# Three-part kernel on one core: 320-long sums in eight full-array passes, and the code for rare inputs moved behind the last block

## The chip, the core and the metric

The kernel runs on one core of a Trainium2 chip. Times are device microseconds from launch to the end of the slowest core, which is the only one here; a profile gives the times of each instruction in one execution, counted from its first instruction. The engines are TensorE (PE; its weight loads are listed as PEld), VectorE (DVE), ScalarE (ACT), GpSimd (POOL) and SyncE (SP), which issues most of the transfers.

## What is computed

Three parts follow each other. A gated linear attention over 4 sequences of 768 tokens gives 3072 rows of 320 numbers. Then a layer of 8 experts works on those rows whose skip score is positive: each such row goes to one expert. Last, a mixture layer takes the maximum of three products and multiplies it with a fourth matrix.

```python
def _moe_ref(x, w_skip, w_gate, w1, w2):          # x: 3072 x 320
    do_compute = x @ w_skip > 0
    xc = x[do_compute]
    e_idx = argmax(xc @ w_gate)                    # 8 experts
    ...
    h = np.maximum(xc[mask] @ w1[e], 0.0)          # 320 -> 1024
    y[mask] = gate_w[mask, None] * (h @ w2[e])     # 1024 -> 320
    out[do_compute] = xc + y

def _moe2_ref(x, w1, w2, w3, w_out):
    h = np.maximum(np.maximum(x @ w1, x @ w2), x @ w3)   # 320 -> 768
    return h @ w_out                                     # 768 -> 320
```

Both first layers, that of the experts and that of the mixture, are sums over 320 numbers. These are the sums that the change rewrites.

## The kernel before

Every factor is split into a high part and a low part (xH and xL, wH and wL), and a product is made of three: high by high, low weights by high, high weights by low. TensorE adds over 128 rows in one pass, so 320 is two chunks of 128 and a rest of 64. The weights hold the rest twice, in rows 0 to 63 and 64 to 127 of chunk 2. `x_parts` puts the high part of the rest of the tokens into rows 0 to 63 of chunk 2 and its low part into rows 64 to 127, so that one pass over 128 rows gives two of the three products of the rest. For the third, `terms` returns a short product of 64 rows: on rows 0 to 63, or, where `odd` is set, on rows 64 to 127, for which `x_parts` writes a second copy of the high part into a fourth chunk (line 264). So a sum is seven passes over 128 rows and one over 64.

The order is written out by hand; each engine takes its instructions in the order of the program. In `mixed_block` (line 308 for all these passes) the sums come in pairs: the first of a pair ends with its short pass, the second begins with its own, so that the two short passes stand next to each other on different halves of the rows and write different PSUM banks (tags pd and ps). In `experts`, `l1` does the same for two slabs of weights, with four short passes in the middle (line 423; the full ones are line 419). A call of `mixed_block` makes 18 sums (six slices f of 128 columns, three matrices), then the second layer (lines 323 to 325). Behind a sum, `post` handles what is finished of the slice before, and through `between` it places the transposes for the next tokens (lines 261 and 262) there, four times in a block that has another behind it: twice between the two sums of a pair, once between two pairs, once in the second layer.

The stages, by the profile: the attention, with one mixture block of 256 tokens (tile ext) woven into its end; eight experts of 256 rows each; a last step of 128 rows for the fullest expert (`few1`, then its second layer `l2`); a mixture block of 256 tokens (tile fx); five mixture blocks of 512 tokens (tiles fxH and fxL).

Between that last step and the mixture block on fx stands code that only some inputs need (lines 574 to 583): each of the five engines reads a number (`cnt_i`, line 574) and jumps over it where the number is zero (line 575), as with these inputs. Where the code is skipped, each engine still carries out a few semaphore instructions, which bring the semaphores to where they would stand behind it; these have line 575 too. `final` then loads the tokens of the first 512-wide blocks (line 273, on SP's queue).

Of the kernel before, what the change touches and what calls it, by code (L numbers as in the profile page):

```python
# [12 lines left out]
I32 = mybir.dt.int32  # L13
# [35 lines left out]
def build(tc, tp, kp, og, gates, w9, w1, w2, m1, m2, out):  # L49
    nc = tc.nc  # L50
    with ExitStack() as top:
# [24 lines left out]
        final(k, top, mp, wts)  # L76
# [167 lines left out]
def terms(xH, xL, wH, wL, c, odd):  # L244

    out = []
    for q in range(2):
        out += [(wH[:, q, c], xH[:, q]), (wH[:, q, c], xL[:, q]), (wL[:, q, c], xH[:, q])]  # L250

    out.append((wH[:, 2, c], xH[:, 2]))
    return out, ((wL[64:128, 2, c], xH[64:128, 3]) if odd else (wL[0:64, 2, c], xH[0:64, 2]))


def x_parts(k, x, xH, xL, c, bank="tr"):

# [6 lines left out]
    nc.scalar.copy(xH[64:128, 3, c], pt[0:64, 2])  # L264
# [11 lines left out]
def mixed_block(k, mp, x, xt, T, tile, between=None, apart=True):  # L276
# [22 lines left out]
    for f in range(6):  # L299
        c = slice(128 * f, 128 * f + 128)  # L300
        ps = []
        for m in range(3):
            p = k.bank("acc", [128, T])
            odd = (3 * f + m) % 2
            tt, short = terms(*xt, mp.H[m], mp.L[m], c, odd)
            tt = [short] + tt if odd else tt + [short]
            for i, (w, z) in enumerate(tt):
                nc.tensor.matmul(p, w, z, start=i == 0, stop=i == len(tt) - 1)  # L308
            ps.append(p)
            post()  # L310
            if m == 2:
                done.append((f, ps))
            yield
# [74 lines left out]

def experts(k, wts, mp):
    tc, nc = k.tc, k.nc  # L390
    X, XT, HT, l1s = {}, {}, {}, []
# [11 lines left out]
    def xprep(e, j):  # L403
        if j == 0:
            XT[e] = (p2.tile([128, 4, ST], F32R, name="xH"), p2.tile([128, 2, ST], F32R, name="xL"))
# [23 lines left out]

    def few1(e, s, xt):  # L430

        odd = s % 2 == 1
        ps = k.bank("acc", [128, SLAB])
        tt, short = terms(*xt, *wts.h1[e, s], slice(0, SLAB), odd)
        tt = [short] + tt if odd else tt + [short]
        for i, (w, x) in enumerate(tt):
            nc.tensor.matmul(ps, x[:, 0:128], w, start=i == 0, stop=i == len(tt) - 1)
        r = p2.tile([128, RW], F32, tag="y", name="r")
        nc.scalar.activation(r[:, 0:SLAB], ps, AF.Relu)
        yield  # L440
        pt = k.bank("tr", [128, 2, 128])
        for f in range(2):
            nc.tensor.transpose(pt[:, f], r[:, 128 * f : 128 * f + 128], k.ident)
        h = hp.tile([128, 2, ST], F32R, tag="hH", name="hH")[:, :, 0:128]
        g = hp.tile([128, 2, ST], F32R, tag="hL", name="hL")[:, :, 0:128]
        nc.scalar.copy(h, pt)
        nc.vector.tensor_sub(g, pt, h.bitcast(F32))
        yield h, g

    def l2(e, hs, c, xrow, apart=True):  # L450

        py = k.bank("row", [128, DM])
        for s in range(4):
            (hH, hL), (wH, wL) = hs[s], wts.h2[e, s]
            for f in range(2):
                a = s == 0 and f == 0
                z = s == 3 and f == 1
                nc.tensor.matmul(py, hH[:, f, c], wH[:, f], start=a, stop=False)
                nc.tensor.matmul(py, hH[:, f, c], wL[:, f], start=False, stop=False)
                nc.tensor.matmul(py, hL[:, f, c], wH[:, f], start=False, stop=z)  # L460
        y = p2.tile([128, RW], F32, tag="y", name="y")
        nc.scalar.copy(y[:, DM:RW], xrow[:, DM:RW])
        nc.vector.scalar_tensor_tensor(y[:, 0:DM], py, xrow[:, GTC : GTC + 1], xrow[:, 0:DM], ALU.mult, ALU.add)  # L463
        ins = nc.gpsimd.indirect_dma_start(  # L464
            k.table, bass.IndirectOffsetOnAxis(ap=xrow.bitcast(I32)[:, PLC : PLC + 1], axis=0), y, None,
            bounds_check=ROWS - 1, oob_is_err=False)
        if apart:
            k.apart(ins, "y", "y", "xl", "last", "pad")

    def more(e, n):  # L470

        with tc.If(n > ST):
            nc.sync.dma_start(k.table[bass.ds(n + e * CAP, 128)], k.zrow)
            for s in range(4):
                wts.raw1(e, s)
                wts.split1(e, s)
            for s in range(4):
                wts.raw2(e, s)
                wts.split2(e, s)
            with tc.For_i(ST, n, 128) as i:  # L480
                xo = p2.tile([128, 2, RW], F32, tag="xb", bufs=3, name="xo")[:, 0]
                nc.sync.dma_start(xo, k.table[bass.ds(i + e * CAP, 128)])
                xt = p2.tile([128, 4, ST], F32R, name="xH"), p2.tile([128, 2, ST], F32R, name="xL")
                x_parts(k, xo, *xt, slice(0, 128))
                hs = []
                for s in range(4):
                    *_, h = few1(e, s, xt)
                    hs.append(h)
                l2(e, hs, slice(0, 128), xo, apart=False)
# [13 lines left out]
    xt = wts.early = [wts.pool[2].tile([128, n, T1], F32R, name=f"fx{n}") for n in (4, 2)]  # L503
    wts.ahead1()
    counts = counted(k)
    for e in range(E + 1):
# [23 lines left out]
        for s in range(4):  # L530
            if e < E:
                HT[e, s] = l1(e, s, XT[e])
            else:
                last = few1(e, s, XT[e])
# [18 lines left out]
        for j in range(nj):  # L553
            l2(e, [HT[e, s] for s in range(4)], slice(128 * j, 128 * j + 128), X[e][:, j])
# [7 lines left out]
    def redo():  # L562

        x = p2.tile([128, 2, RW], F32, tag="xb", bufs=3, name="xo")[:, :, 0:MW]
        mixed_load(k, x, 0, T1)
        mixed_load(k, fx, T1, T1)
        x0 = p2.tile([128, 4, ST], F32R, name="xH"), p2.tile([128, 2, ST], F32R, name="xL")
        for j in range(2):
            x_parts(k, x[:, j], *x0, slice(128 * j, 128 * j + 128))
            x_parts(k, fx[:, j], *xt, slice(128 * j, 128 * j + 128))  # L570
        for _ in mixed_block(k, mp, x, x0, T1, early_tiles(wts, p2), apart=False):
            pass

    rare = nc.values_load(k.cnt_i[0:1, E + 4 : E + 5], min_val=0, max_val=N)
    with tc.If(rare > 0):
        left = nc.values_load(k.cnt_i[0:1, E + 2 : E + 3], min_val=0, max_val=N)
        with tc.If(left > 1):
# [811 lines left out]
```

## Time and profile before

| | us |
|---|---|
| median of 3 runs | 621.68 (618.18 to 624.29) |
| profiled execution, its own time | 618.2 |
| its span, first to last instruction | 616.5 |
| TensorE busy | 584.5 (95%) |
| VectorE, GpSimd, ScalarE busy | 323.9, 261.2, 255.5 |

The profiled execution is at the fast end of the three runs. The mean granted clock of TensorE was 0.987 of its full 2.4 GHz. A pass of TensorE is listed with its whole passage through the array, so that two passes that follow each other overlap in the list; what counts is the distance from one start to the next. A row of the timeline that ends in x2 stands for two passes of one kind.

### The profile page before, as it was taken

What the parts mean: (1) busy time and instruction counts of PE and PEld (TensorE: products, weight loads), DVE (VectorE), ACT (ScalarE), POOL (GpSimd) and SP (SyncE); (2) the same over time, 40 slices, a digit from 0 to 9 for tenths busy, and PEclk for the clock granted to TensorE, in tenths of its full rate; (3) what the DMA queues carried; (4) which work ended last, traced back from release to release, by engine and by line L of the source; (5) the groups of instructions that cost most, each with busy time, mean ns of one, the idle gap of its engine ahead of it and who ended that gap; (6) DMA issues with size and microseconds to landing.
All of it is one profiled execution on the core that took longest, in us unless ns stands there. A gap on an engine that the chain in (4) does not pass through costs nothing. (4 is left out here: it accounts for less than half of the span.)

```text
span 616.5 us, 11321 instructions
## 1 busy us (share of the span) xinstructions
PE 584.5 (95%) x4187; PEld 492.2 (80%) x4187; DVE 323.9 (53%) x792; ACT 255.5 (41%) x563; POOL 261.2 (42%) x281
## 2 busy tenths in 40 slices
PE   7979798899999999999999799999999999999994
PEld 3867687778888999999999687687688778678774
DVE  7889898998976477766666132231230321231220
ACT  4563646464634666666666132231232232222211
POOL 4346576777756555555553112213223123223222
PEclk9999998989999999999999899999999999999998
DMA  8587886787534677777763200002002002001001
GB/s 272 186 286 240 280 258 197 255 263 242 168 107 144 203 247 225 215 230 228 225 208 112 94 2 22 1 1 85 2 0 86 0 1 86 0 1 44 1 0 44
DMA packets 40857, 81.09 MB, mean 132 GB/s; under 512 B 6750, under 2 KB 21983, under 8 KB 40792
## 3 DMA queue, kind: packets, MB, share of 16 engines
q1 hardware_dynamic: 29608, 61.37, 31.5%
q10 hardware_dynamic: 8064, 9.05, 4.9%
q0 software_dynamic: 3120, 9.85, 4.2%
q8 instruction: 36, 0.59, 0.4%
q14 instruction: 29, 0.24, 0.1%
HBM read 66.68 MB, written 14.43 MB: 132 GB/s over the span
## 5 line engine op out<-in xcount | busy, mean ns | idle before, releaser
L287 POOL TENSOR_TENSOR hL<-t,hH 128x512 fp32r<-128x512 f32 x30 | 38.6, 1287 | 148.0 <-ACT hH L286 148.0
L308 PE MATMUL ps<-fxH,mH 128*128 128x512 f32 x135 | 57.7, 428 | 0.0
L308 PE MATMUL ps<-fxH,mL 64*128 64x512 f32 x135 | 57.6, 427 | 0.0
L308 PE MATMUL pd<-fxH,mL 128*128 128x512 f32 x135 | 57.5, 426 | 0.0
L286 ACT CAST hH<-t 128x512 fp32r<-128x512 f32 x30 | 18.6, 621 | 92.3 <-DVE t L296 92.3
L961 PE MATMUL pv<-KP,W 128*128 128x123 f32 (+2 forms) x384 | 53.1, 282 | 0.3 <-DVE xs L968 0.2
L308 PE MATMUL pd<-fxH,mH 128*128 128x512 f32 x135 | 52.9, 392 | 0.0
L961 PEld LDWEIGHTS pv<-KP,W 128*128 128x128 f32 x384 | 47.9, 193 | 3.5 <-DVE xs L968 0.7
L295 DVE TENSOR_TENSOR t<-t,ps 128x512 f32<-128x512 f32 x15 | 10.3, 688 | 65.0 <-PE ps L308 64.9
L981 POOL TENSOR_TENSOR g<-O,den 128x320 f32<-128x320 f32 x24 | 19.3, 804 | 52.6 <-DVE den L978 38.9
L308 PEld LDWEIGHTS pd<-fxH,mL 128*128 128x128 f32 x135 | 25.1, 186 | 19.5 <-issue 15.9
L887 ACT ACTIVATE W<-pd 128x512 f32<-128x512 f32 x48 | 27.6, 591 | 25.9 <-PE pd L886 19.4
L464 POOL DMA_INDIRECT table<-y,xb x17 | 16.7, 985 | 48.8 <-DVE y L463 37.5
L308 PEld LDWEIGHTS ps<-fxH,mH 128*128 128x128 f32 x135 | 25.3, 187 | 15.0 <-issue 11.0
L896 PE MATMUL ps<-TP 64*128 64x128 f32 x384 | 29.4, 291 | 7.1 <-DMA TP<-tp 6.2
L308 PE MATMUL ps<-fxL,mH 128*128 128x512 f32 x90 | 35.5, 395 | 0.0
L330 POOL DMA_INDIRECT out<-o,fx x22 | 21.6, 981 | 32.0 <-ACT o L329 30.1
L308 PE MATMUL pd<-fxL,mH 128*128 128x512 f32 x90 | 35.1, 390 | 0.0
L896 PEld LDWEIGHTS ps<-TP 64*128 64x128 f32 x384 | 24.7, 193 | 11.7 <-DVE mtmp L228 4.2
L904 DVE TENSOR_TENSOR W<-ps,W 128x512 f32<-128x512 f32 x48 | 30.5, 674 | 0.4 <-PE ic L925 0.4
L308 PEld LDWEIGHTS ps<-fxH,mL 64*128 64x128 f32 x135 | 25.1, 186 | 5.5 <-issue 1.6
L308 PEld LDWEIGHTS pd<-fxH,mH 128*128 128x128 f32 x135 | 25.4, 188 | 5.1
(484 smaller groups left out, 1775.1 us busy)
## 6 DMA issues: line engine op xcount, KB each, us to landing
raw<-w SPq DMA_DIRECT2D x36, 384.0 KB
TP<-tp SPq DMA_DIRECT2D x24, 512.0 KB
raw<-w SPq DMA_DIRECT2D x36, 320.0 KB
KP<-kp SPq DMA_DIRECT2D x24, 324.0 KB
mraw<-m ACTq DMA_DIRECT2D x18, 384.0 KB
O<-og SPq DMA_DIRECT2D x6, 640.0 KB
fx<-table SPq DMA_DIRECT2D x5, 642.0 KB
table<-zrow SPq DMA_DIRECT2D x8, 323.0 KB
```

The costliest lines, as they stand in the source:

```text
L286: nc.scalar.copy(h, t)
L287: nc.gpsimd.tensor_sub(g, t, h.bitcast(F32))
L295: nc.vector.tensor_max(t, t, ps[1])
L308: nc.tensor.matmul(p, w, z, start=i == 0, stop=i == len(tt) - 1)
L330: ins = nc.gpsimd.indirect_dma_start(k.out, bass.IndirectOffsetOnAxis(ap=x.bitcast(I32)[:, j + q, IDC : IDC + 1], axis=0), o, None, bounds ...
L464: ins = nc.gpsimd.indirect_dma_start(k.table, bass.IndirectOffsetOnAxis(ap=xrow.bitcast(I32)[:, PLC : PLC + 1], axis=0), y, None, bounds_c ...
L887: nc.scalar.activation(st[i]["W"][:, q], pd, AF.Exp)
L896: nc.tensor.matmul(ps[q][:, j], TP[r, 1, j], TP[r, 0, j], start=True, stop=True)
L904: nc.vector.tensor_mul(t["W"][:, q], t["ps"][q], t["W"][:, q])
L961: nc.tensor.matmul(t["pv"][:, h:h1], t["W"][:, h % 2, h // 2], t["ve"][:, h:h1], start=True, stop=True)
L981: nc.gpsimd.tensor_mul(g, sg[c][:, b], bc(den.unsqueeze(2), [128, H, D]))
```

## The change

The short pass goes: the third product of the rest is now made over all 128 rows of chunk 2, where the weights stand twice and the tokens are high part over low part, so that it also adds low weights by low tokens. Each sum is eight full passes in one fixed order, without `odd`. `l1` makes its two slabs one after the other. `x_parts` no longer writes the second copy, and the tiles for high parts have three chunks, not four. `few1` and `l2` become functions of the module with unchanged work. The code for rare inputs becomes `rare`, called behind `final`; inside, it redoes all blocks of the mixture, where it redid two before.

```diff
@@ build
-        final(k, top, mp, wts)
+        final(k, mp, wts)
+        rare(k, mp, wts)
@@ terms
-def terms(xH, xL, wH, wL, c, odd):
+def terms(xH, xL, wH, wL, c):
     out = []
     for q in range(2):
         out += [(wH[:, q, c], xH[:, q]), (wH[:, q, c], xL[:, q]), (wL[:, q, c], xH[:, q])]
-    out.append((wH[:, 2, c], xH[:, 2]))
-    return out, ((wL[64:128, 2, c], xH[64:128, 3]) if odd else (wL[0:64, 2, c], xH[0:64, 2]))
+    return out + [(wH[:, 2, c], xH[:, 2]), (wL[:, 2, c], xH[:, 2])]
@@ x_parts
     nc.scalar.copy(xH[0:64, 2, c], pt[0:64, 2])
-    nc.scalar.copy(xH[64:128, 3, c], pt[0:64, 2])
     nc.scalar.copy(xH[:, 0:2, c], pt[:, 0:2])
@@ mixed_block
-            odd = (3 * f + m) % 2
-            tt, short = terms(*xt, mp.H[m], mp.L[m], c, odd)
-            tt = [short] + tt if odd else tt + [short]
+            tt = terms(*xt, mp.H[m], mp.L[m], c)
@@ experts, l1
-        odd = s % 2 == 1
-        if not odd:
-            l1s[:] = [(k.bank("acc", [128, 2, ST]),
-                       [terms(*xt, *wts.h1[e, s + i], slice(128 * f, 128 * f + 128), i) for f in range(2)])
-                      for i in range(2)]
-        ps, tt = l1s[odd]
+        ps = k.bank("acc", [128, 2, ST])
         for f in range(2):
-            for i, (w, x) in enumerate(tt[f][0]):
-                nc.tensor.matmul(ps[:, f], w, x, start=not odd and f == 0 and i == 0, stop=odd and f == 1 and i == 6)
-        if not odd:
-            for f in range(2):
-                for i, (p, t) in enumerate(l1s):
-                    nc.tensor.matmul(p[:, f], *t[f][1], start=i == 1 and f == 0, stop=i == 0 and f == 1)
+            for i, (w, x) in enumerate(terms(*xt, *wts.h1[e, s], slice(128 * f, 128 * f + 128))):
+                nc.tensor.matmul(ps[:, f], w, x, start=f == 0 and i == 0, stop=f == 1 and i == 7)
@@ experts, behind the last step
-    rare = nc.values_load(k.cnt_i[0:1, E + 4 : E + 5], min_val=0, max_val=N)
-    with tc.If(rare > 0):
...
@@ behind final
+def rare(k, mp, wts):
+    tc, nc = k.tc, k.nc
+    some = nc.values_load(k.cnt_i[0:1, E + 4 : E + 5], min_val=0, max_val=N)
+    with tc.If(some > 0), ExitStack() as own:
...
```

What this does to the rows of an engine is shown at three places. The first is TensorE in a mixture block of 512 tokens, from the third pass of a first sum into the second sum; fxH and fxL are the tokens, mH and mL the weights, pd and ps the two banks. Before:

```order
L308 MATMUL pd_7343<-fxH_7177,mL0_76 128x512
L308 MATMUL pd_7343<-fxH_7177,mH0_73 128x512
L308 MATMUL pd_7343<-fxL_7178,mH0_73 128x512
L308 MATMUL pd_7343<-fxH_7177,mL0_76 128x512
L308 MATMUL pd_7343<-fxH_7177,mH0_73 128x512
L308 MATMUL pd_7343<-fxH_7177,mL0_76 128x512
L308 MATMUL ps_7352<-fxH_7177,mL1_77 128x512
L308 MATMUL ps_7352<-fxH_7177,mH1_74 128x512
L308 MATMUL ps_7352<-fxL_7178,mH1_74 128x512
```

The same place after the change:

```order
L305 MATMUL pd_5451<-fxH_5289,mL0_76 128x512
L305 MATMUL pd_5451<-fxH_5289,mH0_73 128x512
L305 MATMUL pd_5451<-fxL_5290,mH0_73 128x512
L305 MATMUL pd_5451<-fxH_5289,mL0_76 128x512
L305 MATMUL pd_5451<-fxH_5289,mH0_73 128x512
L305 MATMUL pd_5451<-fxH_5289,mL0_76 128x512
L305 MATMUL ps_5460<-fxH_5289,mH1_74 128x512
L305 MATMUL ps_5460<-fxL_5290,mH1_74 128x512
```

Before, the last pass on pd and the first on ps are the short ones, next to each other; now the pass with mL0 that closes the first sum is a full one, and the second sum begins with its full pass on mH1 and keeps its own pass with mL1 for its end. The count of passes of a pair stays 16.

The second place is TensorE at the end of the experts: `ic` is the last product of the last step, fx the tokens of the block behind it. Before:

```order
L460 MATMUL ic<-w_3H,hL 128x320
L458 MATMUL ic<-w_3H,hH 128x320
L459 MATMUL ic<-w_3L,hH 128x320
L460 MATMUL ic<-w_3H,hL 128x320
L574 TENSOR_LOAD cnt_i
L575 COMPARE_AND_BRANCH
```

The same place after:

```order
L416 MATMUL ic<-w_3L,hH 128x320
L417 MATMUL ic<-w_3H,hL 128x320
L305 MATMUL pd<-fx_3267,mH_73 128x256
L305 MATMUL pd<-fx_3268,mH_73 128x256
L305 MATMUL pd<-fx_3267,mL_76 128x256
```

The read of cnt_i and the branch no longer stand between the experts and the mixture block; the same holds for the four other engines.

The third place is the end of the program on GpSimd, which issues the stores of the result. Before:

```order
L287 TENSOR_TENSOR hL<-t,hH 128x512 x6
L330 DMA out<-o,fx 3072x320 x4
L287 TENSOR_TENSOR hL<-t,hH 128x512 x6
L330 DMA out<-o,fx 3072x320 x4
L1385 UNCONDITIONAL_BRANCH
```

The same place after:

```order
L327 DMA out<-o,fx 3072x320 x4
L286 TENSOR_TENSOR hL<-t,hH 128x512 x6
L327 DMA out<-o,fx 3072x320 x4
L595 TENSOR_LOAD cnt_i
L596 COMPARE_AND_BRANCH
```

The read and the branch now follow the last stores, ahead of the end of the program.

## Rows read from the trace of the kernel before

**Rows 1.** Busy time by stretch: length; PE, PEld, DVE, ACT, POOL; clock; DMA share, GB/s.

```profile
173.90:199.28 25.38, 25.38 (x197) 21.79 (x196) 17.46 (x71) 9.43 (x32) 13.45 (x19) 1.00 0.40 133
...
211.00:331.00 120.00, 120.00 (x909) 115.95 (x908) 82.79 (x130) 74.96 (x158) 64.58 (x46) 1.00 0.71 222
...
420.70:468.27 47.57, 47.57 (x229) 36.71 (x229) 11.09 (x20) 12.21 (x28) 11.65 (x10) 1.00 0.09 28
```

**Rows 2.** Timeline of TensorE, an undivided pair; start us, busy us, what.

```profile
469.49 0.39 PE L308 MATMUL pd<-fxH,mH 128*128 128x512 f32 x1
469.81 0.50 PE L308 MATMUL pd<-fxH,mL 64*128 64x512 f32 x1
469.81 0.50 PE L308 MATMUL ps<-fxH,mL 64*128 64x512 f32 x1
...
470.58 0.39 PE L308 MATMUL ps<-fxL,mH 128*128 128x512 f32 x1
...
471.97 0.39 PE L308 MATMUL pd<-fxH,mH 128*128 128x512 f32 x1
...
473.33 0.39 PE L308 MATMUL pd<-fxH,mH 128*128 128x512 f32 x1
```

**Rows 3.** Timeline of TensorE, a pair divided by transposes, and undivided ones.

```profile
488.65 0.39 PE L308 MATMUL pd<-fxH,mH 128*128 128x512 f32 x1
...
490.64 0.40 PE L308 MATMUL ps<-fxL,mH 128*128 128x512 f32 x1
...
495.86 0.38 PE L261 MATMUL mi<-ident,fx 128*128 128x128 f32 x2
```

**Rows 4.** Timeline of TensorE, 256-wide block behind the experts.

```profile
344.31 0.48 PE L308 MATMUL pd<-fx,mH 128*128 128x256 f32 x2 [3.69 <-DVEq L575]
...
354.55 0.40 PE L308 MATMUL pd<-fx,mH 128*128 128x256 f32 x2
...
355.27 0.28 PE L308 MATMUL pd<-fx,mH 128*128 128x256 f32 x1
...
356.13 0.29 PE L308 MATMUL ps<-fx,mL 128*128 128x256 f32 x1
...
357.45 0.28 PE L308 MATMUL pd<-fx,mH 128*128 128x256 f32 x1
...
359.10 0.29 PE L308 MATMUL ps<-fx,mL 128*128 128x256 f32 x1
```

**Rows 5.** Timeline of TensorE, first layer of an expert.

```profile
236.91 0.28 PE L419 MATMUL pd<-xH,w_0H 128*128 128x256 f32 x1
...
238.46 0.28 PE L419 MATMUL pd<-xH,w_0H 128*128 128x256 f32 x1
...
239.45 0.28 PE L419 MATMUL ps<-xH,w_1L 128*128 128x256 f32 x1
```

**Rows 6.** Instructions of line 575, count, duration ns min/median/max, first and last start.

```profile
L575 PEldq COMPARE_BRANCH  x1: 3388/3388/3388, 339.3 to 339.3; - x1
...
L575 POOLq INC_SWDGE_SEM  x1: 1044/1044/1044, 346.4 to 346.4; - x1
```

**Rows 7.** Busy time in half a microsecond behind the branch, columns as in 1.

```profile
345.00:345.50 0.50, 0.50 (x4) 0.36 (x2) 0.00 (x0) 0.00 (x0) 0.00 (x0) 0.50 0.11 27
```

**Rows 8.** Timeline of GpSimd, the last write into the table.

```profile
341.98 0.99 POOL L464 DMA_INDIRECT table<-y,xb  x1 [7.78 <-DVE y L463]
```

**Rows 9.** Timeline of SyncE, the loads for the 512-wide blocks.

```profile
348.00 1.02 SPq L273 DMA_DIRECT2D fx<-table  x2
```

**Rows 10.** DMA issues: count, KB each, median us to landing.

```profile
table<-y,xb POOLq DMA_INDIRECT x17, 4.2
```

**Rows 11.** Busy time in the last half microsecond with those loads, columns as in 1.

```profile
353.00:353.50 0.50, 0.50 (x6) 0.35 (x4) 0.00 (x0) 0.41 (x1) 0.00 (x0) 1.00 0.39 126
```

**Rows 12.** Timeline of GpSimd, the last store.

```profile
609.26 0.98 POOL L330 DMA_INDIRECT out<-o,fx  x1 [1.71 <-ACT o L329]
```

**Rows 13.** Instructions of line 1385, columns as in 6.

```profile
L1385 POOLq DRAIN  x3: 40/113/6602, 609.0 to 616.2; - x3
```

More of the change, by code (lines that the diff above doesn't have):

```diff
@@ L386, in counted, with few1, l2 @@
     yield
+def few1(k, wts, p2, hp, e, s, xt):
+    nc = k.nc
+    ps = k.bank("acc", [128, SLAB])
+    tt = terms(*xt, *wts.h1[e, s], slice(0, SLAB))
+    for i, (w, x) in enumerate(tt):
+        nc.tensor.matmul(ps, x[:, 0:128], w, start=i == 0, stop=i == len(tt) - 1)
+    r = p2.tile([128, RW], F32, tag="y", name="r")
+    nc.scalar.activation(r[:, 0:SLAB], ps, AF.Relu)
+    yield
+    pt = k.bank("tr", [128, 2, 128])
+    for f in range(2):
+        nc.tensor.transpose(pt[:, f], r[:, 128 * f : 128 * f + 128], k.ident)
+    h = hp.tile([128, 2, ST], F32R, tag="hH", name="hH")[:, :, 0:128]
+    g = hp.tile([128, 2, ST], F32R, tag="hL", name="hL")[:, :, 0:128]
+    nc.scalar.copy(h, pt)
+    nc.vector.tensor_sub(g, pt, h.bitcast(F32))
+    yield h, g
+def l2(k, wts, p2, e, hs, c, xrow, apart=True):
+    nc = k.nc
+    py = k.bank("row", [128, DM])
+    for s in range(4):
+        (hH, hL), (wH, wL) = hs[s], wts.h2[e, s]
+        for f in range(2):
+            a = s == 0 and f == 0
+            z = s == 3 and f == 1
+            nc.tensor.matmul(py, hH[:, f, c], wH[:, f], start=a, stop=False)
+            nc.tensor.matmul(py, hH[:, f, c], wL[:, f], start=False, stop=False)
+            nc.tensor.matmul(py, hL[:, f, c], wH[:, f], start=False, stop=z)
+    y = p2.tile([128, RW], F32, tag="y", name="y")
+    nc.scalar.copy(y[:, DM:RW], xrow[:, DM:RW])
+    nc.vector.scalar_tensor_tensor(y[:, 0:DM], py, xrow[:, GTC : GTC + 1], xrow[:, 0:DM], ALU.mult, ALU.add)
+    ins = nc.gpsimd.indirect_dma_start(
+        k.table, bass.IndirectOffsetOnAxis(ap=xrow.bitcast(I32)[:, PLC : PLC + 1], axis=0), y, None,
+        bounds_check=ROWS - 1, oob_is_err=False)
+    if apart:
+        k.apart(ins, "y", "y", "xl", "last", "pad")
 def experts(k, wts, mp):
     tc, nc = k.tc, k.nc
-    X, XT, HT, l1s = {}, {}, {}, []
+    X, XT, HT = {}, {}, {}
     p2 = wts.x
@@ L428, in l1 @@
         return h, g
[L430 to L489, printed above, removed]
@@ L502, in experts @@
     fx = wts.pool[2].tile([128, 2, MW], F32, name="fx")
-    xt = wts.early = [wts.pool[2].tile([128, n, T1], F32R, name=f"fx{n}") for n in (4, 2)]
+    xt = wts.early = [wts.pool[2].tile([128, n, T1], F32R, name=f"fx{n}") for n in (3, 2)]
     wts.ahead1()
@@ L533, in experts @@
             else:
-                last = few1(e, s, XT[e])
+                last = few1(k, wts, p2, hp, e, s, XT[e])
                 next(last)
@@ L553, in experts @@
         for j in range(nj):
-            l2(e, [HT[e, s] for s in range(4)], slice(128 * j, 128 * j + 128), X[e][:, j])
+            l2(k, wts, p2, e, [HT[e, s] for s in range(4)], slice(128 * j, 128 * j + 128), X[e][:, j])
             if j == 0:
@@ L560, in experts @@
                 wts.ahead2()
[L562 to L572, printed above, removed]
-    rare = nc.values_load(k.cnt_i[0:1, E + 4 : E + 5], min_val=0, max_val=N)
-    with tc.If(rare > 0):
-        left = nc.values_load(k.cnt_i[0:1, E + 2 : E + 3], min_val=0, max_val=N)
-        with tc.If(left > 1):
-            for e in range(E):
-                more(e, nc.values_load(k.cnt_i[0:1, e : e + 1], min_val=0, max_val=N))
-        again = nc.values_load(k.cnt_i[0:1, E + 3 : E + 4], min_val=0, max_val=N)
-        with tc.If(again > 0):
-            redo()
     own.close()
@@ L600, in early_tiles, with final @@
     return tile_
-def final(k, ctx, mp, wts):
+def final(k, mp, wts):
     tc, nc = k.tc, k.nc
-    p2 = ctx.enter_context(tc.tile_pool(name="fi2", bufs=2))
-    hp = ctx.enter_context(tc.tile_pool(name="fih", bufs=8))
+    own = ExitStack()
+    p2 = own.enter_context(tc.tile_pool(name="fi2", bufs=2))
+    hp = own.enter_context(tc.tile_pool(name="fih", bufs=8))
     X, XT = {}, {}
@@ L1157, in early_prep @@
             if j == 0:
-                early["xt"] = tuple(p3.tile([128, n, T1], F32R, tag=t, name="ext") for n, t in ((4, "TP"), (2, "KP")))
+                early["xt"] = tuple(p3.tile([128, n, T1], F32R, tag=t, name="ext") for n, t in ((3, "TP"), (2, "KP")))
             x_parts(k, early["x"][:, j], *early["xt"], slice(128 * j, 128 * j + 128), "acc")
```

44 lines of the change are left out of this document (42 added, 2 removed).

## The prediction

> **What bounds the kernel now.** I first read the busy time by stretch. From the end of the attention to the last block TensorE has no idle time in any stage: 25.38 of 25.38 us while the first mixture block is woven in, 120.00 of 120.00 us in the experts, 47.57 of 47.57 us in a 512-wide block, of which there are five [rows 1]. No other engine is over 70% busy in these. So a microsecond of TensorE's passes taken out here is a microsecond of the program, unless another chain lies just beneath it.
>
> A busy TensorE is not one at its peak, so I then read the starts of its passes. In a 512-wide block full passes follow each other by (473.33 - 471.97) / 6 = 0.227 us in the first sum of a pair and by (471.97 - 470.58) / 6 = 0.232 us in the second, the last of these steps being the hop to the other bank [rows 2]; I use 0.229. Around the short passes it is slower. The two start together at 469.81, so they do run side by side, but from the last full pass ahead of them (469.49) to the second full pass behind them (470.58) it takes 1.09 us [rows 2]: three ordinary steps are 0.69, so the short pair takes 0.40 beyond a step where one full pass takes 0.23. TensorE waits for a switch ahead of the short passes and for another behind them.
>
> Last I looked for idle time, and found one place of over a microsecond: the branch over the code for rare inputs. TensorE idles 3.69 us there [rows 4], and its own branch takes 3.388 us [rows 6]. Behind it the granted clock is 0.50, the 1.2 GHz level [rows 7].
>
> **The 512-wide blocks.** A pair goes from 14 full and two short passes to 16 full ones. The stretch from 469.49 to 470.58 becomes four steps, 4 x 0.229 = 0.92 us: 0.17 us is saved [rows 2]. Where transposes divide a pair, both short passes pay alone: from 488.65 to 490.64 it takes 1.99 us; then four steps and the transposes, for which I take the 0.38 us of an undisturbed row, would be 1.30, so 0.69 is saved [rows 3]. There are 45 pairs in five blocks. Eight are divided (two in each block that has another behind it), 37 are not: 37 x 0.17 + 8 x 0.69 = 11.8 us. The unknown is the step: 720 passes at 0.227 or at 0.232 give 1.9 us more or less, so 9.9 to 13.7.
>
> **The 256-wide block behind the experts.** Its step is (355.27 - 354.55) / 6 = 0.12 us. From 355.27 to 356.13, over one short pair to the third full pass, is 0.86 us against five steps, 0.60: 0.26 saved. Divided, 357.45 to 359.10 is 1.65 against 0.60 + 0.38: 0.67 saved [rows 4]. Seven pairs are undivided and two divided: 3.2 us.
>
> **The block in the attention's end** has the same nine pairs of 256; five are undivided, four are divided by work of the routing. At the same prices that is 5 x 0.26 + 4 x 0.67 = 4.0 us. But here the block fills the time of a chain (routing, scatter, load of the first expert's rows), which does not get shorter. I take 3.0, with 1.0 to 4.0 as bounds: below, only the undivided pairs; above, all.
>
> **The experts.** Four short passes in the middle of two slabs: from 238.46 to 239.45 is 0.99 us; with steps of (238.46 - 236.91) / 13 = 0.119, seven full passes take 0.83, so 0.16 is saved per two slabs [rows 5]. Sixteen times: 2.5 us. Since TensorE has no idle time here [rows 1], I take it whole; the lower bound is 0, if the weights' transfers (222 GB/s in this stretch) turn out to be just hidden. In the last step of 128 rows one pair is undivided and one is divided by transposes that wait for ScalarE: 0.5 us, from 0.26 to 0.9.
>
> **The branch's place.** Without it TensorE goes from the last product of the experts to the block on fx, whose tokens the code loads in the second expert. That is 3.69 us of idle time [rows 4]. It also ends the slow clock: four pairs took 354.55 - 344.31 = 10.24 us, while a pair at full clock takes 0.72 + 0.86 + 5 x 0.12 = 2.18 us, four 8.72 [rows 4]: 1.5 us more. Together 5.2.
>
> What is late next there? The tokens of the first 512-wide block. Before, their load was issued at 348.00 [rows 9], behind the branch's bookkeeping on GpSimd, which ends at 346.4 + 1.04 = 347.4 [rows 6]. Two loads of 642 KB end by 353.5 [rows 11]; with half of that time for the first it lands at some 351. TensorE reaches its first transposes after 11 sums of 8 x 0.12 us: 340.6 + 10.6 = 351.2 in the times of before. The load needs only the last write into the table, issued at 341.98 [rows 8], to land: 4.2 us by the median of these writes [rows 10], so it can be issued at 346.2, and there is 1.7 us of slack. If it were still issued at 348.00, the transposes would come out level or wait some 0.5 us. I take 0, with 0.5 to 1 us as the bound.
>
> **The same branch at the end.** The last store is issued at 609.26 [rows 12]. Before, GpSimd's drain begins at 609.0, takes 6.602 us and so ends at 615.6, close to the end of the span [rows 13]. Now GpSimd reads cnt_i and branches first. In the middle of the program the same sequence ended 347.4 - 341.98 = 5.4 us after the store ahead of it was issued [rows 6, 8]. The drain ended 6.4 us after its store [rows 12, 13]. If the drain is over when what the store set going is over, the branch hides in it and costs about nothing; if the drain takes its 5.4 us after the last instruction of GpSimd (609.26 + 0.98 to 615.6), the end moves by 5.4 - 0.98 = 4.4 us. No row tells these apart. I take 1.0, nearer to the first, because the two other drains of line 1385 take 0.04 and 0.11 us, which is what a drain alone costs [rows 13]. The other engines reach their branch earlier and have room.
>
> **ScalarE's second copy** of the rest is one instruction per `x_parts`, on an engine that is not the bound: nothing.
>
> **The sum.** 11.8 + 3.2 + 3.0 + 2.5 + 0.5 + 5.2 - 1.0 = 25.2 us. The profiled execution took 618.2 us, so it would come to 593.0. It lies 3.5 us below the median of the runs, 621.68; carried over to that, 596.5. I name 595.5, a little towards the profile's own.
>
> **Rivals.** First, **the end takes part of it back**: the drain follows the branch instead of covering it, 4.4 us instead of 1.0. For it speaks that GpSimd takes its instructions in order; against it the two short drains. It gives 596.4 for the profile's execution and some 599 to 600 by the median. The Trainium skill's page "Runtime: NRT & Kernel Launch", section "Instruction fetch mechanics", says that a taken branch whose target lies outside the fetched window must wait for the fetch of that page; by that rule the jump at the end pays as the one in the middle does, and this rival is how the cost would show. TensorE's 3.388 us branch agrees with the rule.
>
> Second, **only the mixture gains**. The weights' transfers or the chain of the routing lie just beneath TensorE in the experts and the attention's end, so 3.0 and 2.5 give almost nothing. Against it: no idle time on TensorE and other engines at 70% or less [rows 1]. That loses 4.5 us: about 600.
>
> Third, **the branch was not what held TensorE**: at 344.31 its wait was ended by VectorE's line 575 [rows 4], and something else of VectorE or ScalarE could take that place. Against it: the row names line 575 itself, which is gone from there, and fx is transposed ahead of the last step. It loses 5.2 us: about 601.
>
> Fourth, on the other side, **the switch was not the short passes' price**. They do run side by side [rows 2], so two passes of 64 rows cost one place of the array, and the change puts in one full pass per pair. If the time around them stayed (because it belonged to the hop from bank to bank, or to the start of a sum), 45 x 0.229 + 18 x 0.12 + 33 x 0.119 = 16.4 us would be added, 5.2 taken off for the branch, and 1.0 added at the end: 12.2 us slower, 634. It decides as soon as a pair without short passes still shows over 0.7 us of extra time. Against it: the hop from ps to pd, which has no short pass, is an ordinary step [rows 2]. The Trainium skill's page "TensorEngine Tiling (Array Packing)", section "Theoretical Speedup", promises up to twice the speed for sums of 64 rows or fewer; by it this change is a loss of that 12.2 us. Its section "Key Properties" says that a change of the tiling mode drains the engine; by that the short pair pays twice, and the trace agrees with this one.
>
> **Chances.** The forecast as worked out 0.52; the end takes part back 0.25; only the mixture gains 0.13; the branch was not the hold 0.06; slower by the fourth rival 0.03; the rest is open. All but the slower one lie between 588 (11.8 and 3.2 at their upper bounds, no cost at the end, from the profile's 618.2) and 605 (two rivals together, from the median). The runs of before differ by 1% among themselves, so 1% is about what this measurement can tell from no change. Faster by over 1% has 0.95, within 1% 0.02, slower 0.03.
>
> **What would show it.** Right: passes of line 305 with even steps of 0.227 to 0.232 us at every hop; a 512-wide block of about 45.0 us instead of 47.57; an expert 0.3 us shorter; no idle time between the experts and the block on fx, and a granted clock of 1.00 there; the load of the first 512-wide block's tokens issued some 4 us after the last write into the table; a last store followed by 6 to 7 us. Wrong: a gap ahead of the first transposes in the block on fx, a gap between the routing and the first expert, a drain that ends over 10 us after the last store, or a step of 0.24 us or more in sums of full passes.

## The result and the profile after

The kernel after takes 595.94 us (median of four runs) against 622.25 for the kernel before beside it: ratio 0.9575, 95% interval 0.9501 to 0.9649. One of the four, 604.65 us, was in a slower state and is not in the ratio. The forecast was 595.5. In a second set of six runs it was 595.81 us, 0.9578 (0.9535 to 0.9621). The profiled execution took 594.08 us (the sum in the prediction gave 593.0), with a span of 592.3; before, these were 618.2 and 616.5.

To see where 24.2 us of span went I took the start of TensorE's first pass of every stage from the timeline of both kernels and subtracted (us):

| stage, from its first pass to the next one's | before | after | change | forecast |
|---|---|---|---|---|
| attention (not touched) | 173.92 | 173.14 | -0.78 | 0 |
| early block of 256 | 31.50 | 28.27 | -3.23 | -3.0 |
| eight experts | 125.24 | 123.62 | -1.62 | -2.5 |
| last step of 128 rows, to its last product | 9.65 | 8.67 | -0.98 | -0.5 |
| to the first pass of the next block | 4.00 | 0.15 | -3.85 | -3.69 |
| block of 256 behind the experts | 28.64 | 23.84 | -4.80 | -4.7 (3.2, and 1.5 by the clock) |
| five blocks of 512, to the last pass | 235.22 | 221.76 | -13.45 | -11.8 |
| last pass to the end of the span | 8.33 | 12.84 | **+4.51** | **+1.0** |

The busy time by stretch, columns as in [rows 1]: most of the experts, one 512-wide block, and half a microsecond where the clock was 0.50 before [rows 7].

```profile
210.00:325.00 115.00, 114.33 (x876) 113.81 (x875) 82.13 (x129) 67.57 (x139) 64.22 (x45) 1.00 0.72 228
402.39:447.06 44.67, 44.67 (x231) 38.79 (x229) 11.08 (x20) 10.76 (x24) 11.68 (x10) 1.00 0.09 30
334.50:335.00 0.50, 0.50 (x6) 0.50 (x6) 0.10 (x1) 0.00 (x0) 0.00 (x0) 1.00 0.00 0
```

A 512-wide block is 2.9 us shorter at the same full busy share, which shows again that busy was not peak. The experts now have 0.67 us without work, and the half microsecond behind the place of the old branch has the full clock.

The timeline of TensorE after (start us, busy us, what, idle time ahead of it):

```profile
212.10 0.42 PE L416 MATMUL ic<-w_2L,hH 128*128 128x320 f32 x1 [0.30 <-POOL w_2L L153]
...
213.62 0.41 PE L416 MATMUL ic<-w_3L,hH 128*128 128x320 f32 x1 [0.37 <-POOL w_3L L153]
...
333.70 0.31 PE L417 MATMUL ic<-w_3H,hL 128*128 128x320 f32 x1
333.85 0.40 PE L305 MATMUL pd<-fx,mH 128*128 128x256 f32 x2
...
344.41 0.38 PE L261 MATMUL pl<-ident,fx 128*128 128x128 f32 x2
...
402.39 0.39 PE L305 MATMUL pd<-fxH,mH 128*128 128x512 f32 x1
...
404.00 0.39 PE L305 MATMUL pd<-fxH,mL 128*128 128x512 f32 x1
404.23 0.39 PE L305 MATMUL ps<-fxH,mH 128*128 128x512 f32 x1
...
406.04 0.39 PE L305 MATMUL pd<-fxH,mH 128*128 128x512 f32 x1
...
407.86 0.39 PE L305 MATMUL ps<-fxH,mH 128*128 128x512 f32 x1
...
422.93 0.39 PE L305 MATMUL ps<-fxL,mH 128*128 128x512 f32 x1
...
424.32 0.39 PE L305 MATMUL ps<-fxH,mL 128*128 128x512 f32 x1
```

From 404.23 to 406.04 and from there to 407.86 it is eight steps each, 0.226 and 0.228 us a step, one sum in each of the two banks; the 0.232 of one of them before [rows 2] is gone there. It was not a property of the bank: the slower step is still found in the first sum behind another kind of pass, in either bank. Behind the second layer it is (404.00 - 402.39) / 7 = 0.230 us in pd, behind transposes (424.32 - 422.93) / 6 = 0.232 in ps, and the sum after that is at 0.227 again.

The block on fx follows the last product by an ordinary 0.15 us, where 3.69 us of waiting stood [rows 4]. The first transposes of the next block's tokens (344.41) wait for nothing. Their load follows GpSimd's last write into the table; the timelines of these two engines:

```profile
335.38 0.99 POOL L421 DMA_INDIRECT table<-y,xb  x1 [6.80 <-issue]
...
580.55 0.98 POOL L327 DMA_INDIRECT out<-o,fx  x1 [1.71 <-ACT o L326]
```

```profile
338.04 0.94 SPq L272 DMA_DIRECT2D fx<-table  x2
```

The load is issued 2.66 us after the write; the forecast took 4.2. The second row above is the last store. What follows it at the end, the instructions of lines 596 and 1384 (columns as in [rows 6]):

```profile
L596 POOLq EVENT_SEMAPHORE  x6: 17/30/43, 583.7 to 584.1; - x6
...
L596 PEldq COMPARE_BRANCH  x1: 3602/3602/3602, 577.6 to 577.6; - x1
...
L596 POOLq COMPARE_BRANCH  x1: 53/53/53, 580.9 to 580.9; - x1
L596 POOLq INC_SWDGE_SEM  x1: 1484/1484/1484, 584.6 to 584.6; - x1
```

```profile
L1384 POOLq DRAIN  x3: 40/107/5383, 586.1 to 592.0; - x3
```

GpSimd is busy with the store until 581.53; its sequencer takes the branch at 580.9 and then does nothing until 583.7. Six semaphore instructions end at 584.19. At 584.55 the store lands, 4.0 us after its issue, and at 584.6 a counting instruction for the skipped transfers (INC_SWDGE_SEM) starts, which takes 1.48 us; the drain starts at 586.1 and takes 5.38. Before, the drain ended 5.4 us after GpSimd was through with the last store; now it ends 5.4 us after the counting, which itself ends 4.5 us after the store. TensorE's own branch, 3.60 us, starts at 577.6 and is hidden.

### The profile page after: what moved, and what is told of

Same layout as the page of the kernel before. It is cut to its first block, busy times and chain, and to the rows that moved or that the text cites. A ratio compares the mean times of both kernels' runs of the same rounds, so it can differ in the third digit from the quotient of the medians.

```text
span 592.3 us, 11259 instructions
## 1 busy us (share of the span) xinstructions
PE 560.7 (95%) x4187; PEld 504.1 (85%) x4187; DVE 322.6 (54%) x792; ACT 241.3 (41%) x522; POOL 262.8 (44%) x281
## 4 chain that ended last, share of the span: by engine, by line
PE 72%; DVE 13%; POOL 4%; DMA 4%; issue 4%; ACT 1%; SPq 0%; POOLq 0%; ACTq 0%; DVEq 0%
PE ps L305 17%; PE pd L305 17%; PE pd L452 5%; PE ps L452 4%; PE pv L960 2%; DMA TP<-tp 2%; PE ic L416 2%; PE ic L417 2%; PE ic L415 2%; PE pv L417 2%; PE pv L416 2%; PE pv L415 2%; DVE mtmp L229 2%; DVE W L903 1%; PE ps L895 1%
## 5 line engine op out<-in xcount | busy, mean ns | idle before, releaser
L305 PE MATMUL ps<-fxH,mH 128*128 128x512 f32 x135 | 53.3, 395 | 0.0
L305 PE MATMUL pd<-fxH,mL 128*128 128x512 f32 x135 | 52.6, 390 | 0.0
L305 PE MATMUL ps<-fxH,mL 128*128 128x512 f32 x135 | 52.6, 390 | 0.0
L305 PEld LDWEIGHTS ps<-fxH,mL 128*128 128x128 f32 x135 | 25.3, 188 | 5.4
```

## The experiments

The attention, which no kernel here touches, took 171.6 to 186.3 us from execution to execution. Behind it a stage that is left alone repeats to 0.1 us, only the first two experts moving (with the new sums from 15.5 to 17.3 and from 15.2 to 15.7 us). So a single profile tells little by its span, and much by its stages. All of them (us; the sum runs from TensorE's first pass of the early block to the end of the span, which is read to 0.1 us, so that the last two columns are good to 0.05):

| kernel | early | experts | last step | gap | 256 | 512s | end | sum |
|---|---|---|---|---|---|---|---|---|
| before | 31.50 | 125.24 | 9.65 | 4.00 | 28.64 | 235.22 | 8.33 | 442.58 |
| move only | 31.50 | 125.24 | 9.65 | 0.14 | 27.11 | 235.22 | 13.20 | 442.06 |
| sums only | 28.26 | 123.41 | 8.68 | 4.23 | 25.40 | 221.76 | 8.33 | 420.08 |
| after | 28.27 | 123.62 | 8.67 | 0.15 | 23.84 | 221.76 | 12.84 | 419.16 |
| after, again | 28.27 | 124.12 | 8.68 | 0.15 | 23.84 | 221.73 | 12.89 | 419.67 |
| no code for other inputs | 28.27 | 124.46 | 8.68 | 0.14 | 23.83 | 221.77 | 8.31 | 415.46 |
| the same, late memsets | 28.30 | 123.79 | 8.70 | 0.15 | 23.85 | 221.73 | 9.23 | 415.75 |
| short body, end | 28.27 | 122.72 | 8.68 | 0.15 | 23.84 | 221.76 | 8.24 | 413.66 |
| short body, middle | 28.26 | 124.04 | 8.68 | 0.46 | 23.92 | 221.77 | 8.26 | 415.37 |
| long body, no GpSimd transfers | 28.27 | 122.56 | 8.68 | 0.14 | 23.83 | 221.77 | 10.44 | 415.69 |
| lone short passes | 34.23 | 146.74 | 9.95 | 0.15 | 30.48 | 257.08 | 13.50 | 492.12 |
| middle, hint late | 28.28 | 123.14 | 9.95 | 4.07 | 25.41 | 221.76 | 8.29 | 420.91 |
| middle, hint early | 29.20 | 122.91 | 8.68 | 1.74 | 23.91 | 221.77 | 8.28 | 416.48 |
| middle, hint early, again | 29.14 | 122.66 | 8.74 | 1.74 | 23.90 | 221.77 | 8.30 | 416.25 |

Six runs stand alone, and their times are not used: lone short passes 665.39 us, late memsets 599.27, short body at the end 595.84 and in the middle 598.62, long body 590.55, early hint for the first time 590.73.

### The two halves of the change, each alone

The sums alone are the kernel before with the new `terms`, `x_parts` and loops of the experts:

```
-def terms(xH, xL, wH, wL, c, odd):
+def terms(xH, xL, wH, wL, c):
...
+    return out + [(wH[:, 2, c], xH[:, 2]), (wL[:, 2, c], xH[:, 2])]
```

> The eight-pass sums as in the kernel after, the code for other inputs left in the middle as in the kernel before. The shape sets the price (theory of the prediction, with the end corrected): the end of the program costs 8.3 us as before, PE waits about 3.9 us at the branch and about 1.5 us go to the low clock behind it, against 4.5 us more at the end in the kernel after; so the profiled span is 592.3 + 5.4 - 4.5 = 593 us, the time about 596 to 597 us, not to be told from the kernel after. Rival, the move as the prediction sized it (end +1.0): 592.3 + 5.4 - 1.0 = 596.7 us of span, time about 600 us. Rival, the gain in the middle was the clock's alone and comes by itself with the full passes: span 588 us.

The move alone is the kernel after with the old `terms` and loops:

```
-        final(k, top, mp, wts)
+        final(k, mp, wts)
+        rare(k, mp, wts)
```

> The code for other inputs behind the last block as in the kernel after, the seven-pass sums with divided short passes as in the kernel before. With the end as measured in the kernel after: 616.5 - 5.4 + 4.5 = 615.6 us of span, time about 621 us, within 1% of the kernel before. By the prediction's end of +1.0: 612.1 us of span, time about 617 us. PE from its last pass to the end of the span: about 12.8 us by the first, about 9.3 us by the second.

Sums only: 598.17 us, ratio 0.9639 (0.9575 to 0.9703). Its span of 596.8 is the number that the rival with the end at +1.0 gave, but by chance: its attention took 176.72 us against 173.14. By the stages it is 0.92 us behind the kernel after, as the expectation with the end corrected had it. Move only: 621.53 us, 0.9982 (0.9942 to 1.0023), no gain that can be measured; by the stages 0.52 us, with the end at 13.20. So the move gives 3.9 to 4.1 us of waiting and 1.5 us of clock and takes 4.5 to 4.9 back at the end. The gain is that of the sums: 22.5 us (442.58 to 420.08). The rows of TensorE's wait and of the branch in the kernel with the sums only:

```profile
341.30 0.47 PE L304 MATMUL pd<-fx,mH 128*128 128x256 f32 x2 [3.92 <-DVEq L559]
```

```profile
L559 DVEq EVENT_SEMAPHORE  x2: 21/21/21, 341.1 to 341.2; - x2
...
L559 PEldq COMPARE_BRANCH  x1: 3423/3423/3423, 336.1 to 336.1; - x1
L559 DVEq COMPARE_BRANCH  x1: 72/72/72, 338.1 to 338.1; - x1
```

They also show whose branch held TensorE. Its own is done at 336.1 + 3.4 = 339.5. VectorE's is 0.07 us long by its row, but VectorE does nothing until 341.1, 3.0 us later, and TensorE starts at 341.30 behind that.

### No code for other inputs

```
         final(k, mp, wts)
-        rare(k, mp, wts)
```

> The kernel after without the code for other inputs: that part of the computation is left out, and the given input does not need it. If the 4.5 us at the end are the branch's, PE's last pass to the end of the span falls back from 12.8 to 8.3 us and the span to 587.8 us, time about 591.5 us (ratio to the kernel before about 0.950). If the prediction's +1.0 was right and the rest of the 4.5 us is the order of the last stores or the drain's own spread, the end stays at 11 to 12 us and the span falls by 1 us only.

The end is 8.31 us, and every other stage that of the kernel after but for the first two experts. So the 4.5 us come with the skipped code: its read, its branch and the bookkeeping behind the branch. The time, 594.53 us, ratio 0.9538 (0.9460 to 0.9615), can't tell this kernel from the kernel after; its profiled execution took 603.46 us, 186.3 of them in the attention, and is used by its stages only.

### What costs the 4.5 us at the end

```
+    for _ in range(3):
+        nc.gpsimd.memset(p2.tile([128, DM], F32, tag="o", name="o", bufs=3), 0.0)
     own.close()
```

> The kernel after without the code for other inputs (left out; the given input does not need it), and with three small memsets on GpSimd behind the last store, over the tiles that the last three stores read, so that the last memset waits until the last store has landed, as GpSimd did at the moved branch. If the 5.4 us drain follows whatever GpSimd instruction is last: the last store lands 4.0 us after its start, 5.1 us after PE's last pass; a memset of some 0.3 us, the drain of 5.4 us and 0.8 us behind it make 11.5 us from PE's last pass to the end of the span. If the drain belongs to the last store and runs beside its flight (rival): 8.3 us as without the memsets.

```profile
L588 POOL MEMSET o<- x3: 382/386/388, 590.3 to 590.9; 128x320 f32 x3
```

```profile
L1385 POOLq DRAIN  x3: 45/107/5967, 590.8 to 597.3; - x3
```

The memsets did not wait as meant: they followed the store at once, and the last one began before it landed. So neither of the two cases expected came about, and the 11.5 was not tried. They still answer: the last memset ends at 590.93 + 0.39 = 591.32, the drain, begun at 590.75, at 596.72, 5.4 us later, and the end is 0.9 us longer for 0.99 us of memsets. The drain's end follows GpSimd's last instruction by 5.4 us, here a memset, before a store.

Next the skipped code was made short, four instructions (a memset, a transpose and two copies) and no transfer, at the end and in the middle; and left long, but with SyncE's transfers in place of GpSimd's scatters:

```
     with tc.If(some > 0), ExitStack() as own:
+        p2 = own.enter_context(tc.tile_pool(name="rah", bufs=1))
+        x = p2.tile([128, 128], F32, name="x")
+        nc.gpsimd.memset(x, 0.0)
...
```

For the long body, in the second layer of the mixture (and likewise in `l2`):

```
+                    if not apart:
+                        nc.sync.dma_start(k.out[128 * (j + q) : 128 * (j + q) + 128], o)
+                        continue
```

> The kernel after with the skipped code cut to four instructions without a transfer (the rest of the code for other inputs is left out). From PE's last pass to the end of the span: about 12.8 us if any branch at the end costs the same; 11.3 us if only the 1.5 us increment of the semaphores for skipped transfers goes and the wait for the last landing stays; 10.5 us if that wait goes too and the 2.8 us after the branch on GpSimd stay; 8.5 to 9 us if those also depend on how far the branch jumps.

> The same four skipped instructions, but where the kernel before has its branch, ahead of the first undivided block (the rest of the code for other inputs is left out). If PE's stop of 3.7 to 3.9 us there was the price of any taken branch: a gap of at least 3.4 us again and 1.5 us more in the block behind it at the low clock. If it was the price of a long jump: a gap under 1 us, the clock not lowered, the 256-wide block 23.8 us. The end of the program 8.3 us in both.

> The kernel after with the skipped code at its full length, but its stores as plain transfers of the sync queue to fixed rows instead of GpSimd's scatters (so the code for other inputs would store to the wrong rows; the given input skips it). If the increment of the semaphores for skipped GpSimd transfers, and the wait for the last landing ahead of it, make the end long: from PE's last pass to the end 10.5 us, with the 2.8 us after the branch on GpSimd left. If the wait for the landing stays without them: 11.3 us. If the length of the jump is all: 12.8 us as in the kernel after.

The branch and the drain with the short body at the end:

```profile
L596 PEldq COMPARE_BRANCH  x1: 223/223/223, 584.0 to 584.0; - x1
...
L596 POOLq COMPARE_BRANCH  x1: 45/45/45, 587.3 to 587.3; - x1
L596 POOLq EVENT_SEMAPHORE  x1: 17/17/17, 587.5 to 587.5; - x1
```

and with the long body without GpSimd's transfers:

```profile
L600 POOLq EVENT_SEMAPHORE  x2: 17/17/17, 582.4 to 582.5; - x2
...
L600 POOLq COMPARE_BRANCH  x1: 53/53/53, 579.8 to 579.8; - x1
```

```profile
L1388 POOLq DRAIN  x3: 44/107/5383, 582.6 to 588.6; - x3
```

With the short body GpSimd's next instruction comes 0.2 us after its branch and TensorE's branch takes 0.22 us; the end is 8.24, as without any branch. With the long body GpSimd loses 2.6 us after the branch, but neither waits for the landing nor counts: 10.44, as expected. So the 4.5 us are about 2.1 of jump (2.6, less what the store's own issue covers) and 2.4 for the skipped transfers: 1.5 of counting, and 0.4 each of four more semaphore instructions and of waiting for the last landing.

What the jump waits for can be seen among the transfers, where those that bring in code are listed as `instruction`. From the branch of GpSimd to the landing in the kernel after (580.8 to 585.0; packets, MB, share; then the stores):

```profile
q0 software_dynamic: 48, 0.16, 11.4%
q14 instruction: 4, 0.03, 2.8%
q8 instruction: 1, 0.02, 2.1%
...
out<-o,fx POOLq DMA_INDIRECT x1, 4.0
```

With the short body at the end, around all its branches but SyncE's and VectorE's (583.9 to 588.0):

```profile
q0 software_dynamic: 96, 0.33, 21.6%
```

Behind the long jump come five transfers of code in 4.2 us (the kernel before has 65 in its whole page), behind the short one none. In the middle it is the same: six from 335.5 to 342.0 with the sums only, none from 341.5 to 344.5 with the short body, behind the branches of TensorE and VectorE. The last store lands 4.0 us after its issue while code comes in, and 2.5 us in the kernel without the rare code; whether the one slows the other was not tried.

In the middle, the short body leaves a gap of 0.46 us, TensorE's branch takes 0.24 us, and the block behind runs at full clock (1.00; 23.92 us). The 3.4 us were the price of a jump over long code, not of a branch. The Trainium skill's page "Runtime: NRT & Kernel Launch", section "Instruction fetch mechanics", says that a taken branch waits for its target's page if that lies outside the fetched window; by that rule a jump within the window has no such wait and a long one has, and the trace agrees (0.2 us against 2.6 to 3.8).

### Lone short passes

```
-    return out + [(wH[:, 2, c], xH[:, 2]), (wL[:, 2, c], xH[:, 2])]
+    return out + [(wH[:, 2, c], xH[:, 2]), (wL[0:64, 2, c], xH[0:64, 2])]
```

> The kernel after, with the last pass of every 320-long sum taken over 64 rows instead of 128 (rows 64 to 127 of it are left out, a part of the low-order correction): as many passes and loads of weights as after, each short one alone between full ones. If a short pass's price is the change of the tile's shape on both sides (0.40 us for a pair in the kernel before): every sum of 512 columns gets longer by about 0.4 us less what a 64-row pass saves, at least +0.2 and at most +0.45 us a sum; 90 such sums give +18 to +40 us in the five 512 blocks alone, span over 612 us. If passes cost by their count (rival): span 592 us, no change in the blocks.

```profile
446.20 0.39 PE L305 MATMUL pd<-fxH,mH 128*128 128x512 f32 x1
446.52 0.50 PE L305 MATMUL pd<-fxH,mL 64*128 64x512 f32 x1
446.95 0.50 PE L305 MATMUL ps<-fxH,mH 128*128 128x512 f32 x1
447.28 0.39 PE L305 MATMUL ps<-fxL,mH 128*128 128x512 f32 x1
```

The timeline of TensorE: from the full pass ahead to the second one behind it is 1.08 us where three steps are 0.68, so 0.40 beyond the step, just what two short passes side by side took [rows 2]. The five 512-wide blocks grow by 35.3 us for 90 sums, 0.39 each; the blocks of 256 by 6.0 and 6.6 for 18 sums each, 0.33 and 0.37; the experts by 23.1 for 64, 0.36. With the number of passes and weight loads unchanged, half the rows in one of eight passes costs 73 us. The price goes with the change of shape, hardly with the columns. The rival of the pass count is out by a wide margin.

### A hint for the long jump

If the stop is the fetch behind a long jump, the old place in the middle can be had without it: a branch prefetch hint on every engine, in the kernel with the sums only.

```
+            with tc.block(name="here"):
+                tc.mark_branch_hint_location("rare", "LikelyTaken", engines=mybir.ALL_ENGINES)
...
-    with tc.If(rare > 0):
+    with tc.If(rare > 0, label="rare"):
```

> The eight-pass sums, the code for other inputs in the middle as in the kernel before, and on every engine a branch prefetch hint for the jump over it, some 9 us ahead of the branch (behind the eighth expert, in a block of its own). If PE's stop at the branch is the fetch of the code behind a long jump, the hint takes it away: PE's gap ahead of the 256-wide block falls from 4.2 us to about 0.5 us as with the short body, the block takes 23.9 us instead of 25.4, the end of the program 8.3 us; from PE's first early-block pass to the end of the span about 415 us, against 419.2 in the kernel after and 420.1 with the same kernel without hints. If the stop is the price of any taken branch over this code, or the hint is spent or overrun before the branch: 420 us, gap 4.2 us.

Without the block of its own, the same hint goes to the program's start (the traces have it at 0.8 to 0.9 us on every engine):

> The same with the hints at the program's start, some 340 us ahead of the branch. If a hint is kept until its branch comes: as with the late hint, gap about 0.5 us, 415 us from PE's first early-block pass to the end. If what was fetched ahead is overwritten by the code that runs in between: gap 4.2 us, 420 us, as without hints.

Late hint, its wait, its branch and the hints themselves:

```profile
340.43 0.48 PE L304 MATMUL pd<-fx,mH 128*128 128x256 f32 x2 [3.76 <-DVEq L561]
```

```profile
L561 DVEq EVENT_SEMAPHORE  x2: 21/21/21, 340.3 to 340.4; - x2
...
L561 PEldq COMPARE_BRANCH  x1: 1141/1141/1141, 335.2 to 335.2; - x1
L561 DVEq COMPARE_BRANCH  x1: 84/84/84, 337.3 to 337.3; - x1
```

```profile
L1371 PEldq BRANCH_PREFETCH_HINT  x1: 50/50/50, 323.2 to 323.2; - x1
...
L1371 DVEq BRANCH_PREFETCH_HINT  x1: 51/51/51, 326.1 to 326.1; - x1
```

Early hint, the same:

```profile
335.04 0.48 PE L304 MATMUL pd<-fx,mH 128*128 128x256 f32 x2 [1.43 <-DVEq L560]
```

```profile
L560 DVEq EVENT_SEMAPHORE  x2: 21/21/21, 334.9 to 335.0; - x2
...
L560 PEldq COMPARE_BRANCH  x1: 921/921/921, 332.3 to 332.3; - x1
L560 DVEq COMPARE_BRANCH  x1: 84/84/84, 334.3 to 334.3; - x1
```

The late hint shortened TensorE's branch from 3.42 to 1.14 us and did nothing for VectorE (337.3 to 340.3, 3.0 us again), so the gap stayed at 4.07: TensorE waits for VectorE. By the rows the two hints came 12.0 and 11.3 us ahead of their branches, not the 9 that were expected. The last step got 1.3 us longer, TensorE waiting there for ScalarE; that the block around the hint holds ScalarE up is likely, but was not tried. Time 598.49 us, ratio 0.9639 (0.9597 to 0.9681), no gain over the same kernel without hints. The early hint, 330 us ahead, worked on both: VectorE's stop is 0.6 us, the gap 1.74, the clock stays up (23.91), the end is 8.28. Not expected was the early block, 0.9 us longer in both of this kernel's profiles. Its rows show where, on VectorE and on TensorE behind it:

```profile
192.63 1.55 DVE L152 TENSOR_TENSOR w_1L<-raw,w_1H 128x768 fp32r<-128x768 f32 x1 [0.25 <-ACT w_1H L151]
```

```profile
194.57 0.50 PE L304 MATMUL ps<-ext,mH 128*128 128x256 f32 x2 [0.46 <-DVE et L293]
```

The same instruction of VectorE takes 0.98 us in the kernel with the sums only. Why it starts late and takes longer here is open.

The kernel with the early hint was timed beside the kernel after:

> The kernel with the hints at the program's start once more, timed beside the kernel after. From PE's first early-block pass to the end of the span 415.5 to 416.5 us again (419.2 in the kernel after), gap ahead of the 256-wide block 1.7 us, end 8.3 us. In the whole time 3 us, 0.5%, less than the kernel after, if the first stage's scatter of several us lets so little be seen: ratio to the kernel before about 0.953, against 0.9575 for after. If the single look was luck of the fetch: the gap is 4 us again and the ratio 0.962.

> The kernel after itself, for the same chip: ratio to the kernel before 0.9575, as measured, within 0.007; from PE's first early-block pass to the end of the span 419.2 us, end 12.8 us, wherever the first stage ends. If the stages behind the first one scatter as much as the first does, which would take the ledger by stages its ground, this sum differs by over 2 us.

Early hint: 593.21 us, ratio 0.9526 (0.9482 to 0.9571). Kernel after: 595.81 us, 0.9578 (0.9535 to 0.9621). By the medians the hinted kernel is 2.6 us faster, by the stages 2.7 to 3.4; the intervals overlap, so the times alone don't prove it. Its code for other inputs is whole.

## Why the prediction was right, and where not

The time was right because the sums were. One term was wrong, the end, by 3.5 us, and that this doesn't show in the time is luck: the 512-wide blocks gave 1.65 us more than forecast, the last step 0.5, and the attention, which nobody touched, was 0.8 shorter in the profiled execution. At the end it was the first rival (chance 0.25) that came, not the forecast as worked out (0.52).

- **The short passes' price.** Right. The switch on both sides costs 0.40 us, for a pair as for one alone; the fourth rival, that the price was of something else, is refuted by the lone short passes.
- **The 512-wide blocks.** Mis-sized, inside the bounds: 13.45 against 11.8. By the starts of the pairs, the 37 undivided ones gave 0.202 us each and not 0.17, the 8 divided ones 0.744 and not 0.69: 7.5 + 6.0. Most of the miss is the step: 0.229 was the mean of two banks and was kept for the sums after, but most of these go at 0.227. The slower step belongs to the sum behind another kind of pass, so it went where the short pass went. What makes it slower was not tried. (The bound for the step should read 720 x 0.0025 = 1.8, not 1.9.)
- **The 256-wide block.** Right on both terms: at full clock 27.11 us with the old sums and 23.84 with the new ones, 3.27 (3.2 forecast), and 28.64 - 27.11 = 1.53 by the clock (1.5).
- **The early block.** 3.23 against 3.0, inside 1.0 to 4.0. (Five undivided pairs alone would be 5 x 0.26 = 1.3, not 1.0.)
- **The experts.** Mis-sized: 1.62 against 2.5. The price was right: from the second expert on it is 2.20 us in seven experts, as 2.5 x 7/8 says. The first one got 0.58 us longer, waiting twice for the low parts of its second weights from GpSimd (rows at 212.10 and 213.62). "No idle time" was true of the stretch as a whole and did not say how near the next chain was at its first microseconds.
- **The last step.** Mis-sized and outside its bounds: 0.98 against 0.5, from 0.26 to 0.9. By the starts of its pairs the undivided one gave 0.27 and the divided one 0.72, as much as in the mixture: the wait for ScalarE, which was to take part of that, did not.
- **The branch's place.** The sizes were right, 3.85 and 1.53. The third rival is refuted: nothing took its place, and the tokens' load came in time, issued 2.66 us after the last write and not some 4. But the price stood beside the wrong row: TensorE's own 3.388 us branch would have been over earlier, and it was VectorE's jump, which the row of [rows 4] names, that held it.
- **The same branch at the end.** This step failed: "I take 1.0, nearer to the first, because the two other drains of line 1385 take 0.04 and 0.11 us". It was 4.5, the first rival's 4.4. The first drain is not like the other two: it ends 5.4 us after GpSimd's last instruction, be that a store, a memset or the counting behind a branch. The prediction's own sign for this came, a drain that ends over 10 us after the last store: 586.09 + 5.38 - 580.55 = 10.9. In that rival's own terms, the jump and the wait for the landing now stand ahead of the drain instead of under it.

So the move, put at 5.2 - 1.0 = 4.2 us, was worth 0.5 to 0.9, and the sums, put at 21.0, gave 22.5.

## What to carry to other kernels

A pass of another shape between full ones has a price of its own, to be read from the starts of the full passes around it: here a short pass had to save 0.40 us, nearly two full passes, before it paid. Moving skipped code to the end only moves its jump, and the engine with the longest way from its last instruction to the end of the program (GpSimd here) pays nearly all of it; look for the jump's length, since short code is skipped for 0.2 us, and try a prefetch hint before a move. When a stage that nobody touched scatters by more than the effect, compare stage by stage.

## Not expected of the hardware

- A long jump's cost doesn't show in the branch's row on VectorE and GpSimd: 0.05 to 0.08 us there, and the next instruction 2.6 to 3.1 us later. On TensorE the row itself has 3.4 to 3.8 us.
- GpSimd's long drain at the end ends 5.4 us after its last instruction. In the long body without its transfers, the store landed 4.3 us before the drain's end, so it is not the landing that it waits for.
- Skipping code that holds GpSimd transfers costs GpSimd a wait until its last transfer has landed (0.4 us here), and a counting instruction of 1.04 to 1.48 us.
- A prefetch hint given 330 us ahead still worked on TensorE and VectorE, one given 11 to 12 us ahead on TensorE alone. Why the later one failed on VectorE stays open, and no run shows what the hint sets going.
